# Four moves of small work in a fused forward-and-backward kernel: scalings of dO, sorted copies, the first FFT piece, and the order of tiles in pass two

## The chip, the cores and the metric

The kernel runs on one core of one Trainium2 chip. The metric is the time of one execution on the device in microseconds (us), the median of several runs; lower is better. A core has five engines with instruction streams of their own, each executed in order: PE (TensorE, matrix products), DVE (VectorE), ACT (ScalarE), POOL (GpSimd) and SP (SyncE). SP, POOL and ACT also issue DMA transfers. Engines wait for one another through semaphores.

## What is computed

The reference is a forward pass and its gradient. The input x has 2048 rows and 576 columns; the hidden width is F = 4608.

```python
g = sigmoid((x * gate_w).sum(-1, keepdims=True))
a = irfft2(rfft2(x) * (w_r + 1j * w_i))              # spectral branch A
b = (gelu(x @ w_gate) * (x @ w_up)) @ w_down         # gated branch B
out = g * a + (1 - g) * b
# returned: out, and the gradients of sum(out * grad_out) for
# x, w_r, w_i, w_gate, w_up, w_down, gate_w
```

Both branches read the same x; the input B_x is not used. Below, dO is `grad_out`.

## The kernel before, in words

**Tiling.** The 2048 rows are T = 16 row tiles of 128. The hidden width is cut into NG = 18 groups of 256 columns (`FG`). x, dO and their transposes (`xn`, `dB`, `xT`, `dOT`) stay in on-chip memory.

**Pass one** has 18 groups of four steps. A step (g, m) handles row tiles 4m to 4m+3 of group g; its number is `pr` = 4g + m, from 0 to 71, so the "fifth step" is pr 4. In each step PE first computes z = dO w_downᵀ (`H_mm`, lines 462 and 467) into a PSUM tile `z`. ACT copies z out in four instructions scaled by 1 - g (`H_da`, line 490, tile `da`). PE then computes x w_gate and x w_up in two halves (`xy_full`, lines 471 and 478), and ACT copies each half in three instructions (`H_act`, lines 497, 499 and 500, tiles `q`, `xb`, `hu`). DVE forms the gelu and its derivative in `H_ew1` and `H_ew2` (lines 505 to 546), with sigmoids on ACT (lines 525, 528, 529). The results A and dH are stored to DRAM scratch (`scr`) through SP.

**W products.** Behind its own products each step runs a share of the weight-gradient products of the group before (`W_units`): `u_dwd` (line 590: A by dB, for w_down) and `u_dw` and `tail` (lines 608 and 622: xn by dH). PSUM pool `pw` has two buffers `wps`; ACT copies them out (line 559). `u_dwd` needs dB scaled row by row with 1 - g. That is `scale_dB(k, engine)`: four instructions for row tiles 4k to 4k+3, on DVE (line 979) or ACT (line 977). Quarters 0, 1 and 2 are scaled in step 4, quarter 3 in step 5, ahead of two `build_R`.

**FFT pieces.** The transforms of x and dO are cut into units in the list `fft`, taken out in order by `fft_next()`. For each of 16 row tiles of x, and then of dO, there is a first unit `u1` (line 652: six products of the sorted row `xq` with a table `Rt`; ACT copies `Z` out, line 655 or 657) and a second `u2` (line 666; ACT copies `ve` out, line 672; DVE folds, SP stores). All these products use `pftile()`, the same single PSUM buffer (pool `pz`, one buffer, tag "z") as the z of each step: a piece must wait for da, and the next step's z must wait for the piece's copy. `want(pr)` is how many units are due by the end of step pr: none until step 7, one there, three by step 8, then three a step. In a step, the first piece (`k0`) goes between the two row tiles of the second half of xy, the others among the W products at due places.

**Sorts.** `sort(dst, t)` is one ACT instruction that copies row tile t, its columns regrouped into six classes, into `xq` (lines 720 and 722; for dO it is scaled by g and reads `graw`, loaded by SP). Before, tiles 0, 1 and 2 of x are sorted in steps 5, 6 and 7 behind `H_act`; the others hang on every odd unit of the list (`sorted_after`), so ACT sorts directly behind that unit's copy.

**Pass two** reads A and dH back, transposed by DMA, as tiles `pin` (line 1142; pool of six), on SP. A job "b" (row tile t) is 72 products of A with `wd_all` for the forward output; "g" and "u" are 72 products each of dH with the transposed w_gate and w_up for the gradient of x, accumulated in the same pair of PSUM buffers (pool `pacc`, eight). The list `jobs` is g0, g1, ten b tiles, u0, u1, b10, and then g, u, b in turn. `load_wuT` (line 1175) loads w_up transposed in nine DMA transposes on SP, one at the start of each job from job 3 on (g0 is job 0); u0 is the first job that needs them. Between the blocks of 12 products of a job, `tick` lets pieces of the inverse transforms run (lines 1269 and 1279, copied out by ACT at lines 1271 and 1281); `posts` joins a finished b tile with its inverse transform on DVE.

Of the kernel before, what the change touches and what calls it, by code (L numbers as in the profile page):

```python
# [20 lines left out]
P, T = 128, 16  # L21
# [9 lines left out]
NG = FF // FG  # L31
# [260 lines left out]
def kernel(  # L292
# [194 lines left out]
    def H_da(g, m, z):  # L487
        da = ewt("da", g)
        for t in range(4):
            nc.scalar.activation(da[:, t, :], z[:, t % 2, t // 2, :], ACT.Copy, scale=omg32[:, 4 * m + t:4 * m + t + 1])  # L490
        return da
# [151 lines left out]
    def fwd_units(src, dst, scale):  # L643
        zs = {}
        CLS = (1, 2, 0, 5, 4, 3)

        def u1(t):
            def f():
                zps = pftile()
                row = src.pop(t)  # L650
                for k, r in enumerate(CLS):
                    nc.tensor.matmul(zps[0:96, k // 3, k % 3 * P:(k % 3 + 1) * P], lhsT=row[:, r], rhs=tb.Rt[t], start=True, stop=True)  # L652
                zs[t] = unit([2, 3 * P], name="Z")
                if scale is None:
                    nc.scalar.copy(zs[t][0:96], zps[0:96, :, 0:3 * P])
                else:
                    nc.scalar.activation(zs[t][0:96], zps[0:96, :, 0:3 * P], ACT.Copy, scale=scale)
            return f

        def u2(t):  # L660
            def f():
                Z = zs.pop(t)
                vps = pftile()
                w = 2 * LQ
                for k in range(6):
                    nc.tensor.matmul(vps[:, k // 3, k % 3 * w:(k % 3 + 1) * w], lhsT=Z[0:96, k // 3, k % 3 * P:(k % 3 + 1) * P],  # L666
                                     rhs=tb.F[0:96, k].rearrange("p c l -> p (c l)"), start=True, stop=True)
                Vt = half([2, DF], name="Vt")
                ve = unit([2, 3, 2, LQ], F32, name="ve")
                sd = unit([2, 3, 2, LQ], F32, name="sd")  # L670
                M = unit([6, 2, LQ], F32, name="vm")
                nc.scalar.copy(ve[:].rearrange("p b k c l -> p b (k c l)"), vps[:, :, 0:3 * w])
                lo, hi = ve[:, 0], ve[:, 1]
                V.tensor_tensor(sd[:, 0], lo, hi, op=ALU.add)
                V.tensor_tensor(sd[:, 1, :, 0], hi[:, :, 0], lo[:, :, 0], op=ALU.subtract)
                V.tensor_tensor(sd[:, 1, :, 1], lo[:, :, 1], hi[:, :, 1], op=ALU.subtract)
                e, o = sd[:, 0, 2], sd[:, 1, 2]
                for k, op in enumerate((ALU.add, ALU.subtract)):
                    V.tensor_tensor(M[:, k], sd[:, 0, 0], sd[:, 0, 1], op=op)
                    V.tensor_tensor(M[:, 4 + k, 1::-1], sd[:, 1, 0], sd[:, 1, 1], op=op)  # L680
                p_, m_ = M[:, 0], M[:, 1]
                for c, op in enumerate((ALU.subtract, ALU.add)):
                    V.scalar_tensor_tensor(M[:, 2, c], m_[:, c], 0.5, o[:, c], op0=ALU.mult, op1=op)
                V.scalar_tensor_tensor(M[:, 3], p_, -0.5, e, op0=ALU.mult, op1=ALU.add)
                up = Vt[:, :, 96:DF - 1].rearrange("p c (j l) -> p j c l", j=2)[:, :, :, 0:LQ]
                dn = Vt[:, :, 1:193].rearrange("p c (j l) -> p j c l", j=2)[:, :, :, 94:47:-1]
                V.tensor_tensor(Vt[:, :, 0:LQ], e, p_, op=ALU.add)
                V.scalar_tensor_tensor(Vt[:, 0, DF - 1:DF - LQ:-1], o[:, 0, 0:LQ - 1], -1.0, m_[:, 0, 0:LQ - 1], op0=ALU.mult, op1=ALU.subtract)
                V.tensor_tensor(Vt[:, 1, DF - 1:DF - LQ:-1], m_[:, 1, 0:LQ - 1], o[:, 1, 0:LQ - 1], op=ALU.subtract)
                for c in range(2):  # L690
                    V.scalar_tensor_tensor(up[:, :, c], M[:, 4:6, c], SIN60, M[:, 2:4, c], op0=ALU.mult, op1=ALU.add)
                for c, s_, op in ((0, -SIN60, ALU.add), (1, SIN60, ALU.subtract)):
                    V.scalar_tensor_tensor(dn[:, :, c], M[:, 4:6, c, 1:LQ - 1], s_, M[:, 2:4, c, 1:LQ - 1], op0=ALU.mult, op1=op)
                LD.dma_start(dst[:, t], Vt[:])
            return f
        return [u1(t) for t in range(T)], [u2(t) for t in range(T)]

    xq, gq, graw = {}, {}, {}

# [16 lines left out]
    def sort(dst, t):  # L716
        if t % 2 == 0:
            classes(dst, t // 2)
        if dst is xq:
            nc.scalar.copy(xq[t], xn[:, t, :].rearrange("p (q r) -> p r q", r=6))  # L720
        else:
            nc.scalar.activation(gq[t], graw[t // 2][:, t % 2].rearrange("p (q r) -> p r q", r=6), ACT.Copy, scale=g32[:, t:t + 1])
# [150 lines left out]
    VC, AC = V.tensor_copy, nc.scalar.copy  # L873
# [27 lines left out]

    early = {2 * T + 4 * k - 13: load_g(k) for k in range(T // 2)}

    def sorted_after(u, n):
        def f():
            u()
            sort(*n)
        return f
    fg = []
    for i, u in enumerate(zipped(*fwd_units(xq, scr_x, None)) + zipped(*fwd_units(gq, scr_g, SD2))):  # L910
        if i in early:
            fg.append(early[i])
        n = (i + 5) // 2
        fg.append(sorted_after(u, (xq, n) if n < T else (gq, n - T)) if i % 2 and n < 2 * T else u)
    mid = mid_units()
    fft = fg + [turned] + mid

# [16 lines left out]
    def ready():  # L934
        u = fft[fft_pos[0]]
        return not hasattr(u, "needs") or u.needs()

    n_mid = sum(1 for u in mid if not getattr(u, "noslot", False))
    n_slots = sum(1 for u in fft if not getattr(u, "noslot", False))
    mid_at = 4 * T + 8  # L940
    NPR = NT // 2
# [4 lines left out]
    def want(pr):  # L946

        n0 = FIRST[-1]
        if pr < len(FIRST):
            return FIRST[pr]  # L950

        def load(n):

            return n + 0.5 * min(max(n - mid_at, 0), n_mid)
        share = load(n0) + (load(n_slots) - load(n0)) * (pr + 1 - len(FIRST)) / (LASTP - len(FIRST))
        n = n0
        while n < n_slots and load(n + 1) <= share + 1e-9:
            n += 1
        return int(min(n, n_slots) + 1e-9)

    wgT_all = []

# [11 lines left out]
    def scale_dB(k, cp):  # L974
        for t in range(4 * k, 4 * k + 4):
            if cp == AC:
                nc.scalar.activation(dB[:, t, :], dB[:, t, :], ACT.Copy, scale=omg32[:, t:t + 1])
            else:
                V.tensor_scalar(dB[:, t, :], dB[:, t, :], omg32[:, t:t + 1], None, op0=ALU.mult)  # L979

    for g in range(NG):
# [3 lines left out]
        for m in range(NPR):  # L985
            pr = g * NPR + m
            n = want(pr) - done[0]
# [65 lines left out]
            else:  # L1053
                z, xy_full = H_mm(g, m)
                da = H_da(g, m, z)
                for f in inside:
                    f()
                xy = xy_full(0)
                if held:
                    held.pop()()  # L1060
                k0 = int(n > 0 and pr > 6 and ready())
                xy0 = xy
                H_act(0, xy0, tiles, 1)
                pcopy[0] = VC
# [4 lines left out]
                    H_act(1, xy, tiles, part)  # L1069
                if pr == 4:  # L1070
                    scale_dB(2, AC)
                elif pr == 5:
                    sort(xq, 0)
                elif pr == 6:
                    next(makeB)
                    sort(xq, 1)
                elif pr == 7:
                    sort(xq, 2)
                state += [*H_ew1(g, tiles, da), da]
                if pr == 4:  # L1080
                    scale_dB(0, VC)
                    scale_dB(1, VC)
                elif pr == 5:
                    scale_dB(3, VC)
                    build_R(nc, tb, unit, 8)
                    build_R(nc, tb, unit, 12)
                side_work(4.4)
# [54 lines left out]
        LD.dma_start_transpose(tl[:], scr[k][t // 4][t % 4][:, f0 * P:(f0 + FCB) * P])  # L1142
        return tl

    jobs = [("g", t) for t in range(2)] + [("b", t) for t in range(10)] + [("u", t) for t in range(2)] + [("b", 10)]
    for t in range(2, T):
        jobs += [("g", t), ("u", t)] + ([("b", t + 9)] if t + 9 < T else [])
    jobs[-2:] = [("x", T - 1)]
    seq = [(k, t, f0) for kind, t in jobs for k in ((1, 2) if kind == "x" else ("bgu".index(kind),)) for f0 in range(0, NFC, FCB)]
    loaded = {}  # L1150
# [28 lines left out]
    with tc.tile_pool(name="p2f", bufs=3, **kw) as p2f, \  # L1179
# [236 lines left out]
                x_out(t, h, pre, o1, LD)  # L1416

        for i, (kind, t) in enumerate(jobs):
            if i > 2 and wT_loads:
                load_wuT(*wT_loads.pop(0))  # L1420
            if kind == "b":
                b_job(t)
                posts()
            elif kind == "g":
                x_half(t, 1)
            elif kind == "u":
                x_half(t, 2)
                need(t)
                assert posted[0] > t
                x_end(t)  # L1430
            else:
                need(t)
                assert posted[0] > t
                gate_grad()
                x_last(t)
# [30 lines left out]
```

## Time and profile before

| what | value |
|---|---|
| runs shown | 1369.44, 1373.15, 1372.83 us; median 1372.83 |
| the profiled execution | 1370.35 us; span of its instructions 1368.5 us |
| granted TensorE clock | 1.00 |
| PE busy, 40 to 905 us (steps of pass one) | 859.22 of 865.00 us |
| PE busy, 920 to 1040 us (start of pass two) | 118.88 of 120.00 us |
| PE busy, 1040 to 1366 us (rest of pass two) | 324.70 of 326.00 us |
| ACT busy, 75 to 100 us | 22.91 of 25.00 us |
| DVE busy, 50 to 75 us | 23.85 of 25.00 us |
| sort of x: L720 ACT COPY, 16 of them | mean 998 ns |
| sort of dO: L722 ACT ACTIVATE, 16 of them | mean 1084 ns |
| DMA share, 920 to 1040 us | 1.13 |

"Busy" is the time in which an engine has an instruction of its own in work. PE's products overlap one another in the pipeline, so the duration of one product is longer than the distance from its start to the next: a product of 512 columns has a duration of 380 ns, while 24 of them take 5.18 us in the chain of waits, 216 ns each. Where this text speaks of lost time on PE, it is worked out from the starts in the timeline and from these distances, not from durations.

### The profile page before, as it was taken

How to read it: one execution, taken by the hardware profiler on the slowest of the kernel's cores; microseconds unless marked ns; L12 is line 12 of the kernel's file. 1: busy time of each engine (PE TensorE's matmuls, PEld its weight loads, DVE VectorE, ACT ScalarE, POOL GpSimd, SP SyncE). 2: the span in 40 equal slices, each digit the busy share in tenths (PEclk: the TensorE clock that was granted, in tenths of full speed). 3: DMA queues.
4: the chain of work that ended last, by engine and by line, in shares of the span. 5: the costliest groups of instructions: out<-in, count | busy, mean ns of one | idle time of the engine just before them, and what ended most of it. 6: DMA issues, size and time to landing. Idle time of an engine off the chain costs nothing.

```text
span 1368.5 us, 27031 instructions
## 1 busy us (share of the span) xinstructions
PE 1355.7 (99%) x10360; PEld 900.7 (66%) x10360; DVE 880.7 (64%) x2353; ACT 772.9 (56%) x1378; POOL 245.1 (18%) x488
## 2 busy tenths in 40 slices
PE   9899999999999999999999999999999999999999
PEld 6456656656655655655655655558887888888887
DVE  7968888888857967876876755525535443545320
ACT  6788887887767776776777666622332322223210
POOL 3011111111222633433433311000000000000000
PEclk9999999999999999999999999999999999999999
DMA  8624435444454644644644657499999888778773
GB/s 224 173 62 136 124 109 153 122 128 128 130 144 117 169 122 132 169 117 120 175 127 126 162 119 183 119 262 205 197 203 216 173 161 169 160 161 175 151 151 75
DMA packets 493465, 206.90 MB, mean 151 GB/s; under 512 B 313332, under 2 KB 485303, under 8 KB 493335
## 3 DMA queue, kind: packets, MB, share of 16 engines
q1 hardware_dynamic: 467188, 170.32, 54.5%
q0 software_dynamic: 15040, 24.38, 6.3%
q10 hardware_dynamic: 11106, 10.48, 3.2%
q8 instruction: 81, 1.33, 0.4%
q14 instruction: 50, 0.40, 0.1%
HBM read 41.04 MB, written 89.11 MB: 95 GB/s over the span
## 4 chain that ended last, share of the span: by engine, by line
PE 94%; DVE 2%; ACT 2%; DMA 1%; issue 0%; SPq 0%; POOL 0%; ACTq 0%; DVEq 0%; POOLq 0%
PE acc L1216 30%; PE xy L478 17%; PE wps L608 17%; PE wps L590 10%; PE z L462 9%; PE wps L622 2%; PE xy L471 2%; PE z L467 2%; PE pf L652 1%; PE acc L1269 1%; DMA wuT<-in_B_w_up_dram 1%; PE acc L1279 1%; PE pf L849 1%; PE pf L771 1%; PE pf L666 1%; DMA pin<-scr 0%
## 5 line engine op out<-in xcount | busy, mean ns | idle before, releaser
L1216 PEld LDWEIGHTS <-pin 128*128 128x128 bf16 x3456 | 334.7, 98 | 85.2 <-issue 2.4
L478 PE MATMUL xy<-wgu,xT 128*128 128x512 bf16 x1152 | 270.5, 380 | 0.0
L608 PE MATMUL wps<-dH,xn 128*128 128x512 bf16 x1152 | 265.3, 379 | 0.0
L608 PEld LDWEIGHTS <-xn 128*128 128x128 bf16 x1152 | 111.3, 98 | 125.7 <-issue 0.6
L478 PEld LDWEIGHTS <-xT 128*128 128x128 bf16 x1152 | 105.6, 98 | 133.1 <-issue 25.9
L590 PE MATMUL wps<-dB,A 128*128 128x288 bf16 x1152 | 150.5, 286 | 3.2 <-DVE dB L979 3.2
L1216 PE MATMUL acc<-wuT,pin 128*128 128x288 bf16 x1152 | 146.4, 286 | 1.4 <-DMA wuT<-in_B_w_up_dram 1.0
L615 POOL DMA_DIRECT2D out_dram<-dw x134 | 72.6, 545 | 416.2 <-ACT dw L559 404.3
L1216 PE MATMUL acc<-wd_all,pin 128*128 128x288 bf16 x1152 | 146.9, 286 | 0.0
L1216 PE MATMUL acc<-wgT,pin 128*128 128x288 bf16 x1152 | 146.6, 286 | 0.0
L1281 ACT ACTIVATE yo<-acc 128x288 bf16<-128x288 f32 x64 | 67.4, 1246 | 132.9 <-PE acc L1279 121.5
L462 PE MATMUL z<-wdT,dOT 128*128 128x256 bf16 x1152 | 137.7, 273 | 0.8 <-DMA wdT<-in_B_w_down_dram 0.7
L590 PEld LDWEIGHTS <-A 128*128 128x128 bf16 x1152 | 111.8, 98 | 36.8 <-issue 4.0
L490 ACT ACTIVATE da<-z,omg 128x256 bf16<-128x256 f32 x288 | 111.9, 471 | 34.7 <-PE z L467 34.6
L462 PEld LDWEIGHTS <-dOT 128*128 128x128 bf16 x1152 | 112.3, 98 | 22.6 <-DMA wdT<-in_B_w_down_dram 1.2
L1397 DVE TENSOR_TENSOR b16t<-acc,f32t 128x288 bf16<-128x288 f32 x32 | 14.7, 458 | 172.9 <-PE acc L1216 172.8
L499 ACT CAST xb<-xy 128x512 bf16<-128x512 f32 x144 | 84.8, 589 | 48.6 <-PE xy L478 47.9
L1271 ACT CAST Z<-acc 98x384 bf16<-98x384 f32 x64 | 27.5, 481 | 106.1 <-PE acc L1269 106.1
L500 ACT CAST hu<-xy 128x512 bf16<-128x512 f32 x144 | 87.0, 604 | 0.0
L497 ACT ACTIVATE q<-xy 128x512 bf16<-128x512 f32 x144 | 80.0, 600 | 3.3 <-PE xy L478 3.3
L536 DVE TENSOR_TENSOR xb<-xb,sg 128x1024 bf16<-128x1024 bf16 x48 | 33.2, 691 | 74.3 <-ACT sg L528 74.3
L559 ACT CAST dw<-wps 128x512 bf16<-128x512 f32 x72 | 42.2, 588 | 48.2 <-PE wps L608 37.0
(515 smaller groups left out, 1811.2 us busy)
## 6 DMA issues: line engine op xcount, KB each, us to landing
scr<-dH SPq DMA_DIRECT2D x144, 256.0 KB, 3.5
scr<-A SPq DMA_DIRECT2D x72, 256.0 KB, 2.6
out_dram<-dw POOLq DMA_DIRECT2D x134, 64.0 KB, 1.9
wd_all<-in_B_w_down_dram SPq DMA_DIRECT2D x3, 1728.0 KB, 13.8
out_dram<-dwd POOLq DMA_DIRECT2D x34, 144.0 KB, 2.7
scr_p<-Vt SPq DMA_DIRECT2D x32, 144.5 KB, 3.4
Vp<-scr_p ACTq DMA_DIRECT2D x32, 144.5 KB, 4.4
wgu<-in_B_w_gate_dram SPq DMA_DIRECT2D x18, 256.0 KB, 4.2
```

Source lines behind the costliest of these rows:

```text
L462: nc.tensor.matmul(zo(t), lhsT=dOT[:, ci, t, :], rhs=wdT[:, ci, :], start=(t % 4 < 2 and ci == 0), stop=False)
L478: nc.tensor.matmul(xy[k][:, t % 2, :], lhsT=xT[:, ci, t, :], rhs=wgu[:, ci, :], start=False, stop=(ci == 3))
L490: nc.scalar.activation(da[:, t, :], z[:, t % 2, t // 2, :], ACT.Copy, scale=omg32[:, 4 * m + t:4 * m + t + 1])
L497: nc.scalar.activation(q[:, h, :], xy[:, :, 0:FG], ACT.Square)
L499: nc.scalar.copy(xb[:, h, :], xy[:, :, 0:FG])
L500: nc.scalar.copy(hu[:, h, :], xy[:, :, FG:2 * FG])
L559: wcopy[0](out, in_)
L590: nc.tensor.matmul(wps[:, :288], lhsT=tl(0, t)[:, fch * P:(fch + 1) * P], rhs=dB[:, t, h * 288:(h + 1) * 288], start=(t == 0), stop=(t == ...
L608: nc.tensor.matmul(wps[:].rearrange("p a b -> p (a b)"), lhsT=xn[:, t, c * P:(c + 1) * P], rhs=kt[t // 4][1][:, t % 4].rearrange("p k f -> ...
L615: wst[0].dma_start(ov[:, c, fsl], dw[:, k, :])
L1216: nc.tensor.matmul(acc[:, :288], lhsT=src[:, r, :], rhs=w_of(r)[:, h * 288:(h + 1) * 288], start=(first and r == 0), stop=(last and r == F ...
L1281: nc.scalar.activation(yv[:, 3 * b:3 * b + 3], ps[:, 0:288].rearrange("p (r q) -> p r q", r=3), ACT.Copy, scale=(SD2, 1.0)[w])
```

## The change

It makes five edits. (1) `scale_dB(3, VC)` moves from step 5 to step 4, so that DVE scales quarters 0, 1 and 3 there in one go. (2) The sorts leave the units and steps 5 to 7; `sort_ahead(pr)` runs directly behind `H_da` of each step and sorts every row tile whose first unit is due in the next step. (3) The first piece of step 7 no longer goes between the halves of xy (`pr > 7` instead of `pr > 6`) but among the W products. (4) Twelve b tiles instead of ten stand ahead of u0. (5) Jobs 5 and 11, counted from 0, load no part of w_up.

```diff
-        return [u1(t) for t in range(T)], [u2(t) for t in range(T)]
+        first = [u1(t) for t in range(T)]
+        for t, u in enumerate(first):
+            u.sort = (src, t)
+        return first, [u2(t) for t in range(T)]
...
-    def sorted_after(u, n):
-        def f():
-            u()
-            sort(*n)
-        return f
...
-        n = (i + 5) // 2
-        fg.append(sorted_after(u, (xq, n) if n < T else (gq, n - T)) if i % 2 and n < 2 * T else u)
+        fg.append(u)
...
+    slots = [u for u in fft if not getattr(u, "noslot", False)]
+    sorted_to = [0]
+
+    def sort_ahead(pr):
+        to = want(pr + 1) if pr + 1 < NG * NPR else n_slots
+        for u in slots[sorted_to[0]:to]:
+            if hasattr(u, "sort"):
+                sort(*u.sort)
+        sorted_to[0] = max(to, sorted_to[0])
...
                 da = H_da(g, m, z)
+                sort_ahead(pr)
...
-                k0 = int(n > 0 and pr > 6 and ready())
+                k0 = int(n > 0 and pr > 7 and ready())
...
-                elif pr == 5:
-                    sort(xq, 0)
                 elif pr == 6:
                     next(makeB)
-                    sort(xq, 1)
-                elif pr == 7:
-                    sort(xq, 2)
                 state += [*H_ew1(g, tiles, da), da]
                 if pr == 4:
                     scale_dB(0, VC)
                     scale_dB(1, VC)
+                    scale_dB(3, VC)
                 elif pr == 5:
-                    scale_dB(3, VC)
...
-    jobs = [("g", t) for t in range(2)] + [("b", t) for t in range(10)] + [("u", t) for t in range(2)] + [("b", 10)]
+    jobs = [("g", t) for t in range(2)] + [("b", t) for t in range(12)] + [("u", t) for t in range(2)] + [("b", 12)]
     for t in range(2, T):
-        jobs += [("g", t), ("u", t)] + ([("b", t + 9)] if t + 9 < T else [])
+        jobs += [("g", t), ("u", t)] + ([("b", t + 11)] if t + 11 < T else [])
...
-            if i > 2 and wT_loads:
+            if i > 2 and i % 6 != 5 and wT_loads:
```

In the order of instructions of the two built programs, every engine has the same work before and after. Step 6 and step 7 hold one sort each; the steps from 8 to 27 hold two and one in turn (two in every even step), all behind da.

## The prediction

> **What bounds the kernel now.** I read the page first, its busy times and the shares of the chain that ended last.
>
> ```profile
> PE 1355.7 (99%) x10360; PEld 900.7 (66%) x10360; DVE 880.7 (64%) x2353; ACT 772.9 (56%) x1378; POOL 245.1 (18%) x488
> ...
> PE 94%; DVE 2%; ACT 2%; DMA 1%; issue 0%; SPq 0%; POOL 0%; ACTq 0%; DVEq 0%; POOLq 0%
> ```
>
> PE is the bound and hardly ever stands still: 1368.5 - 1355.7 = 12.8 us of the span, of which the start and the end take some 4.7 (first product at 1.37 us, last end 3.3 us before the span's). No edit removes products, so the change can only gain what PE waits for, or add waits. The view of PE's waits says for what (waiter, releaser, total us, times, longest):
>
> ```profile
> PE wps L590 <- DVE dB L979: 3.2, 1, 3.2
> ...
> PE acc L1216 <- DMA wuT<-in_B_w_up_dram: 1.0, 1, 1.0
> PE pf L652 <- ACT da L490: 0.9, 1, 0.9
> PE pf L652 <- ACT ve L672: 0.8, 4, 0.2
> ...
> PE acc L1216 <- DMA pin<-scr: 0.4, 1, 0.4
> ```
>
> Each edit stands against one of these rows. I price them from the starts in the timeline, since a wait costs more than its idle time. Distances without a wait: 0.1225 us for a product of 288 columns (48 in 5.88 us in the chain), 0.216 for one of 512.
>
> **Edit 1, dB.**
>
> ```profile
> 59.74 2.61 PE L590 MATMUL wps<-dB,A 128*128 128x288 bf16 x20
> 65.58 2.10 PE L590 MATMUL wps<-dB,A 128*128 128x288 bf16 x12 [3.23 <-DVE dB L979]
> 67.52 1.91 PE L462 MATMUL z<-wdT,dOT 128*128 128x256 bf16 x16
> ```
>
> Twenty products need 20 x 0.1225 = 2.45 us, so the next was due at 62.19 and came at 65.58: 3.39 lost. The last twelve took 1.94 us instead of 1.47, because DVE frees dB tile by tile: 0.47. Together 3.86. In DVE's timeline the eight scalings of step 4 run from 55.94 to 58.17, when the next instruction starts, 0.28 us each; the four of step 5 start only at 65.17, behind the gelu of two steps. Moved up, they end at about 59.3, and PE wants them at 62.2: the wait is gone. Everything behind them on DVE comes 4 x 0.29 = 1.2 us later in step 4 and is level again where they stood. The sigmoid of step 5 waits for that DVE chain: it could start at 65.5 instead of 68.01 (it stood behind a copy that waited for PE), so ACT still moves up. Gain 3.86.
>
> What is late next? DVE's chain in steps 5 and 6 has no idle time to give and ends only some 0.6 us earlier (73.4 against 74.0), while PE is 3.9 ahead. Its consumer on ACT, the sigmoid of step 6, waits behind the two table loads and six sine instructions that begin with ACT's copy at 77.98; DVE's input to it ends at 77.5, the sigmoid starts at 84.76. That slack of 7 us covers it. If it did not, up to 3.3 of the 3.86 would come back.
>
> By the Trainium skill (TensorE: Matmul & The Clock Gate, "What's actually happening") an idle window of about 3.4 us halves PE's clock; a pause of 3.23 us lies just under it. The granted clock is 1.00 in the stretch from 50 to 75 us, so nothing is added here; by the rule at most one window at half speed, an estimate of 1.7 us, would be gained on top.
>
> **Edit 3, the first piece of step 7.**
>
> ```profile
> 83.69 2.76 PE L478 MATMUL xy<-wgu,xT 128*128 128x512 bf16 x12
> 87.32 0.49 PE L652 MATMUL pf<-Rt,xq 128*96 128x128 bf16 x6 [0.86 <-ACT da L490]
> ```
>
> In later steps the piece starts 2.60 after such a row begins (94.57 to 97.17), here 3.63: 1.03 lost, since da was late behind the tables. Four products of 512 later (0.86 us) it would barely have fitted, and the sort that goes from ahead of ACT's copy at 77.98 helps by half a microsecond: gone, +1.03. But there is a new wait. The piece's copy Z now stands on ACT behind da (1.42), one sort (0.9), and six copies of xy (about 2.9), before 0.8 of its own: some 0.5 us after PE wants to write the z of step 8 into the same buffer. PE's next instructions all stand behind that z. Bounds: 0, if da is early, to 1.5. I take 0.5.
>
> **Edit 2, the sorts.** Step 11, PE and ACT:
>
> ```profile
> 137.66 1.89 PE L608 MATMUL wps<-dH,xn 128*128 128x512 bf16 x8
> 139.70 0.49 PE L652 MATMUL pf<-Rt,xq 128*96 128x128 bf16 x6
> ```
> ```profile
> 135.69 1.00 ACT L720 COPY xq<-xn 128x576 bf16<-128x576 bf16 x1
> 136.59 1.07 ACT L497 ACTIVATE q<-xy 128x512 bf16<-128x512 f32 x2
> ...
> 138.97 0.68 ACT L672 COPY ve<-pf 128x588 f32<-128x588 f32 x1
> ```
>
> Eight products need 1.73 us, so the piece was due at 139.39; it waited 0.31 for ve, which ended at 139.65. The sort at 135.69 takes 0.90 of ACT's line ahead of it. Behind da it falls into 0.69 us in which ACT idled for xy, so ve ends about 0.9 earlier. Every fourth step has the same wait: at 139.70, 191.44, 243.25, 295.07 and 346.88, by the same count 0.31, 0.32, 0.39, 0.40, 0.39. Gain 1.8.
>
> The other side: in even steps two sorts (1.8 us, for dO 2.0) now stand ahead of the copies of xy, and behind those wait the pieces' copies, each of which the next piece on PE needs. In steps 10, 14, ... ACT idles 1.46 us there for xy, so little is pushed. Steps 12, 16, 20, 24 are tight: ACT idles only 0.21 (146.29). ACT's line is 1.6 later; ve ends at about 149.4, wanted at 149.82; Z ends at about 152.0, wanted at 151.88. So 0.1 to 0.3 lost in each, 0.7 in all. Bounds: 0, and one sort (0.9) in each of the ten two-sort steps, 9 us.
>
> By the Trainium skill (ScalarE: Activation LUTs, "What ACT_TABLE_LOAD costs") such an instruction of 576 columns would take 186 + 0.833 x 576 = 666 ns. The rows say 998 and 1084 (regrouped reads), and the measurement decides; by the page all the sort terms would shrink by a third.
>
> **Edits 4 and 5, pass two.**
>
> ```profile
> 1037.33 1.14 PE L1216 MATMUL acc<-wuT,pin 128*128 128x288 bf16 x8
> 1039.45 2.12 PE L1216 MATMUL acc<-wuT,pin 128*128 128x288 bf16 x16 [0.97 <-DMA wuT<-in_B_w_up_dram]
> 1042.01 1.65 PE L1216 MATMUL acc<-wuT,pin 128*128 128x288 bf16 x12 [0.45 <-DMA pin<-scr]
> ```
> ```profile
> 948.79 2.98 SPq L1175 DMA_TRANSPOSE wuT<-in_B_w_up_dram  x1
> ...
> 1031.52 3.98 SPq L1175 DMA_TRANSPOSE wuT<-in_B_w_up_dram  x1
> ```
>
> Lost at u0: 1.14 + 0.60 = 1.74. PE takes (1031.11 - 937.36) / 10 = 9.4 us per b tile. SP takes 10.6 with a w_up load (957.56 to 1031.52 is seven tiles) and, without its 3.8, 6.8. So SP falls back by 1.2 per tile: 2.1 us behind the start of its tile at the first load, 9.8 at the last. The last part lands 7.9 (the median) after issue, 17.7 after b9's start, and is wanted at 16.6. Now two tiles carry no load and give back 2.6 each: by the same count the lag is at most 8 and 6.6 at the last load, in b11, landing at 14.5, 2.1 us in time. Gain 1.74. Two short waits on PE among the b tiles, 0.30 (piece at 997.74) and 0.16 (row at 1020.07), come from ACT's own DMA issues standing still between such loads; I count 0.2 of them as gained. Two more tiles run while g0 and g1 hold four of eight PSUM buffers: the ten before lost 0.46 there, so at most 0.1 more.
>
> **Sum.** 3.86 + 1.03 + 1.81 + 1.74 + 0.2 - 0.5 - 0.7 - 0.1 = 7.3 us. The profiled execution took 1370.35 (span 1368.5 and 1.85 around it): 1363.0. The median of the runs is 2.5 higher and would give 1365.5. I take 1364.5.
>
> **The rivals.**
> - ACT and DVE can't follow the earlier PE in steps 6 to 8. For: DVE's chain gains only 0.6. Against: the 7 us of slack ahead of the sigmoid. 3.3 us come back: 1367.8.
> - Pass two keeps a wait at u0, because SP's lag is set by the DMA share (1.13 from 920 to 1040 us), not by the loads alone. Against: 2.1 us of margin. 1.7 come back: 1366.2.
> - The sorts land on the path, the slower end. Place: ACT between da and the copies of xy, in steps 8 to 27. If each of these 20 steps loses one sort of 0.9 to 1.0 us, 19 us are added and the 1.2 counted above for small waits fall away: 1364.5 + 19 - 1.2 = 1382. It decides from about 0.6 us per step on, since 7.3 + 4.1 us must be eaten. For: ACT is busy 22.91 of 25 us from 75 to 100. Against: it idles for xy in most steps, and the sorts removed stood in the same line a few instructions later.
> - The change moves waits without removing them (da late for the piece wherever it stands): 1.0 back, 1365.5, inside the range.
>
> **How the numbers follow.** What a measurement can tell is 0.3%, 4.1 us: faster is below 1368.7. Chances: forecast with its small variants 0.73; first rival 0.11; second 0.10; sorts on the path 0.06. Range 1361 to 1369.5: below, the gain without the new waits (8.6) from the lowest of the profiled and shown times, 1369.4; above, the first two rivals with the upper bound of the run-to-run spread. Faster 0.82 (the first rival falls on both sides of the line), same 0.12, slower 0.06.
>
> **What would show it.** PE's waits without DVE dB, without da at L652 and without wuT at u0; no wait for ve in steps 11, 15, ...; a new short wait of z (L462) for Z at about 87 us less 3.9. The span of PE from its first product to the end of step 71 should shrink by some 5.4, pass two by 1.9. Wrong would be: z or pieces waiting for ACT in most steps from 8 to 27, or u0 waiting for w_up again.

## The result, and the profile after

| | before | after |
|---|---|---|
| median of the runs | 1372.86 us (1369.44 to 1373.15, 4 runs) | 1364.03 us (1362.93 to 1364.56, 4 runs) |
| profiled execution | 1370.35 us, span 1368.5 | 1364.56 us, span 1362.8 |

The ratio of the times is 0.994, with a 95% interval of 0.9923 to 0.9958: faster, by 8.8 us between the medians. It was measured again later, on another chip, in more rounds: 1362.92 us against 1372.58, ratio 0.9929 [0.9916, 0.9941]. The forecast of 1364.5 holds. Between the two profiled executions the difference is only 5.8 us; why the medians are further apart is the main thing that the experiments had to settle.

First the page of the kernel after, its busy times and the shares of the chain that ended last:

```profile
PE 1355.2 (99%) x10360; PEld 901.8 (66%) x10360; DVE 880.8 (65%) x2353; ACT 770.1 (57%) x1378; POOL 246.0 (18%) x488
...
PE 96%; ACT 2%; DVE 1%; DMA 1%; issue 0%; SPq 0%; ACTq 0%; DVEq 0%
```

The work of every engine is what it was; only the span is shorter, and DVE's share of the chain fell from 2% to 1%. The view of PE's waits (waiter, releaser, total us, times, longest):

```profile
PE pf L881 <- POOL ident masks.py:199: 1.4, 1, 1.4
PE pf L433 <- DMA dB<-in_grad_out_dram: 1.2, 1, 1.2
PE acc L1210 <- ACT dw L559: 0.4, 1, 0.4
PE pf L666 <- ACT Z L657: 0.4, 2, 0.2
PE xy L471 <- ACT hu L500: 0.3, 1, 0.3
PE z L462 <- DMA scr<-A: 0.3, 1, 0.3
```

Gone are all five rows of the kernel before that the prediction named: dB, da, ve, wuT and pin. New are the second pieces' wait for Z and one of z (L462), whose releaser is misnamed, as an experiment shows. The first two rows belong to the start of the program, which no edit touches.

PE's timeline in step 4 shows the 20 + 12 products of before as one row, without a pause; DVE's shows the twelve scalings in one go (start, us, engine, line, operation, count):

```profile
61.45 4.08 PE L590 MATMUL wps<-dB,A 128*128 128x288 bf16 x32
65.37 1.91 PE L462 MATMUL z<-wdT,dOT 128*128 128x256 bf16 x16
```
```profile
58.06 3.44 DVE L986 TENSOR_SCALAR dB<-dB,omg 128x576 bf16<-128x576 bf16 x12
```

And step 11, which the prediction showed with its wait for ve, PE and ACT:

```profile
134.86 1.89 PE L608 MATMUL wps<-dH,xn 128*128 128x512 bf16 x8
136.59 0.50 PE L652 MATMUL pf<-Rt,xq 128*96 128x128 bf16 x6
```
```profile
129.83 0.48 ACT L490 ACTIVATE da<-z,omg 128x256 bf16<-128x256 f32 x1
130.19 1.02 ACT L723 COPY xq<-xn 128x576 bf16<-128x576 bf16 x1
...
135.32 0.66 ACT L672 COPY ve<-pf 128x588 f32<-128x588 f32 x1
```

The sort stands behind da, ve ends 0.6 us before the piece, and the piece follows its eight products after 1.73 us, which is their unstalled distance.

Where the time went, stretch by stretch. Every product loads weights, and the starts of these loads are recorded without a gap in every profile (10360 of them); counting them gives the same point of the work in two programs. A point is named below by its time in the first profile of the kernel before. (Some later profiles lack records of a few dozen products, so that PE's busy time there is short by some 7 us.)

| stretch, by the times of before | before, us | after, us | difference | predicted |
|---|---|---|---|---|
| 0 to 45.05, the start | 45.05 | 46.75 | +1.70 | none |
| to 80.02, steps 3 to 6 | 34.97 | 31.11 | -3.86 | -3.86 (dB) |
| to 95.01, steps 7 and 8 | 14.99 | 14.41 | -0.58 | -1.03 + 0.5 |
| to 905.07, the rest of pass one | 810.06 | 809.27 | -0.79 | -1.81 + 0.7 |
| to the last load at 1364.74, pass two | 459.67 | 457.44 | -2.23 | -1.74 - 0.2 + 0.1 |

Without the first row it is 7.46 us, where 7.34 were forecast. The first row doesn't look like the change's doing: no edit touches that stretch, and in twelve other profiles the same point lies at 44.6 to 47.0 us, with no relation to the edits that shows: 46.79 in a second profile of the kernel after, 45.20 in one with edit 5 undone. The windows of after show one stretch at half speed there, from 7.95 to 11.36 us, that the profiled execution of before lacks (start and end, us, busy us and instructions of PE, PEld, DVE, ACT and POOL, granted clock as a share of TensorE's full speed, DMA share, GB/s):

```profile
4.54:7.95 3.41, 2.13 (x34) 1.65 (x32) 1.41 (x3) 0.96 (x4) 1.99 (x6) 1.00 0.95 289
7.95:11.36 3.41, 3.41 (x28) 2.88 (x26) 0.68 (x2) 1.01 (x1) 0.00 (x0) 0.50 1.10 369
```

In the window before it PE stood still for a load of dO (the 1.2 in the waits). In both measurements of the kernel after, the profiled execution is the slowest and the only one with a mean granted clock of 0.999; the other seven have 1.000 and took 1362.4 to 1364.3 us. So the two profiled executions differ by the change and by what happened at the start.

### The profile page after: what moved, and what is told of

The parts are those of the page before. It is cut to its first block, busy times and chain, and to the rows that moved or that the text cites. A ratio compares the mean times of both kernels' runs of the same rounds, so it can differ in the third digit from the quotient of the medians.

```text
span 1362.8 us, 27025 instructions
## 1 busy us (share of the span) xinstructions
PE 1355.2 (99%) x10360; PEld 901.8 (66%) x10360; DVE 880.8 (65%) x2353; ACT 770.1 (57%) x1378; POOL 246.0 (18%) x488
## 4 chain that ended last, share of the span: by engine, by line
PE 96%; ACT 2%; DVE 1%; DMA 1%; issue 0%; SPq 0%; ACTq 0%; DVEq 0%
PE acc L1219 31%; PE xy L478 17%; PE wps L608 17%; PE wps L590 10%; PE z L462 9%; PE wps L622 2%; PE xy L471 2%; PE z L467 2%; PE acc L1272 1%; PE pf L652 1%; PE pf L666 1%; PE acc L1282 1%; PE pf L852 1%; PE pf L774 1%; DMA dB<-in_grad_out_dram 0%; ACT da L490 0%
## 5 line engine op out<-in xcount | busy, mean ns | idle before, releaser
L462 PE MATMUL z<-wdT,dOT 128*128 128x256 bf16 x1152 | 138.6, 274 | 0.3 <-DMA scr<-A 0.3
L462 PEld LDWEIGHTS <-dOT 128*128 128x128 bf16 x1152 | 112.8, 98 | 22.1 <-issue 0.6
## 6 DMA issues: line engine op xcount, KB each, us to landing
wd_all<-in_B_w_down_dram SPq DMA_DIRECT2D x3, 1728.0 KB, 14.9
```

What stands on the lines that cost most here:

```text
L462: nc.tensor.matmul(zo(t), lhsT=dOT[:, ci, t, :], rhs=wdT[:, ci, :], start=(t % 4 < 2 and ci == 0), stop=False)
```

## The experiments

Each kernel ran beside runs of the kernel before on the same chip; ratios are against those.

**The kernel before, unchanged (before_again).**

> The kernel before, unchanged, for a second profile. Between the two profiled executions the change gained 5.8 us (1370.35 to 1364.56), between the medians 8.8. Theory A: the executions of the kernel before differ by how long u0 waits for w_up, since SP's lag of 9.8 us stands just past the point from which PE waits; then a profile here that takes about 1373 shows more than 1.7 us lost at u0 and the same 3.9, 1.0 and 1.8 elsewhere. Theory B: they differ at the start, in the first 45 us, where loads are awaited; then the difference stands there. Theory C: it is spread over all stages.

Measured: 1372.84 us against 1372.58, ratio 1.0001 [0.9991, 1.0011]; profiled 1373.87 us, span 1372.1. Its waits:

```profile
PE wps L590 <- DVE dB L979: 3.6, 1, 3.6
PE acc L1216 <- DMA pin<-scr: 2.1, 2, 1.2
...
PE acc L1216 <- DMA wuT<-in_B_w_up_dram: 0.7, 1, 0.7
```

In pass two it took 461.41 us from 905.07's point to the last load, 1.74 more than the first profile: PE waits now 0.7 for w_up and 2.1 for pin, 3.3 us by starts against 1.74. So the wait at u0 varies from execution to execution of the kernel before, as the theory had it. But 3.5 us separate the two profiled executions, and pass two has half of it. The other half stands in two views, the timeline of PE and the windows from 63.65 us on:

```profile
65.69 2.68 PE L590 MATMUL wps<-dB,A 128*128 128x288 bf16 x12 [3.64 <-DVE dB L979]
68.16 3.04 PE L462 MATMUL z<-wdT,dOT 128*128 128x256 bf16 x16
```
```profile
60.23:63.64 3.41, 1.82 (x15) 1.31 (x14) 3.36 (x6) 2.28 (x4) 0.53 (x2) 1.00 0.75 191
63.65:67.06 3.41, 1.37 (x8) 0.72 (x8) 3.33 (x8) 0.21 (x1) 0.00 (x0) 1.00 0.63 186
67.06:70.47 3.41, 3.41 (x17) 2.34 (x16) 2.23 (x5) 1.54 (x3) 0.54 (x1) 0.50 0.08 32
70.47:73.88 3.41, 3.41 (x48) 2.48 (x46) 3.34 (x7) 1.57 (x4) 0.00 (x0) 1.00 0.05 16
```

The sixteen products of z take 3.04 us where the first profile had 1.91. For exactly 3.41 us after the pause for dB the granted clock is 0.50. From the first product behind the pause to a fixed point after it (69 weight loads) PE takes 8.30 us here and 6.63 in the first profile: 1.67 us that the wait's own length doesn't contain.

**Edit 1 alone (dB_alone).**

```diff
                     scale_dB(1, VC)
+                    scale_dB(3, VC)
                 elif pr == 5:
-                    scale_dB(3, VC)
```

> The kernel before with only the fourth quarter of dB scaled in step 4. Mine: 3.9 us less than the kernel before, and no wait for DVE dB. Rival (ACT and DVE cannot follow the earlier PE): PE waits again in steps 6 to 8, for da at L652 above all, longer than the 0.86 us before, and 0.6 to 2 us are gained.

Measured: 1367.58 us (1366.56 to 1369.33), ratio 0.9967 [0.9955, 0.9979], 5.0 us less by medians; span 1364.7. Its waits:

```profile
PE pf L652 <- ACT ve L672: 1.0, 5, 0.2
PE pf L652 <- ACT da L490: 0.9, 1, 0.9
PE acc L1216 <- DMA wuT<-in_B_w_up_dram: 0.8, 1, 0.8
```

The wait for dB is gone, the others stay as they were: nothing of it comes back behind ACT or DVE, and the first rival falls. The surplus over 3.9 is of the size of the clock's term. The executions with a mean granted clock of 1.000 bear that out: the five of dB_alone took 1367.4 us in the mean and the three of the kernel before beside it 1370.8, only 3.4 more. In this profile the sigmoid of step 6 starts at 81.05, 4.3 us after DVE's input to it ends (76.71).

**Edits 4 and 5 alone (pass2_alone).** The kernel before with the new list of jobs and the skipped loads.

> The kernel before with only twelve b tiles and the two jobs without a load of w_up. Mine: no wait for w_up at u0 and no short waits behind ACT among the b tiles, 1.7 to 2.2 us less in the profile. If theory A on the kernel before holds, 3 to 5 us less by the medians. Rival (SP stays behind because the DMA share is full): a wait for w_up or pin of a microsecond remains at u0, less than 1 us gained.

Measured: 1369.69 us, ratio 0.9979 [0.997, 0.9988], 2.9 us less; span 1366.2. PE waits neither for wuT nor for pin, and pass two takes 457.44 us, as in the kernel after. This profile also shows what the pause for dB hides: it came to 45.05's point 1.05 us later than the first profile (a wait for w_down), waited only 2.1 us for dB, and resumed at 65.52 against 65.58. So in the kernel before a late start can be swallowed by that pause; without the pause it is paid.

**Edits 2 and 3 alone (sorts_alone).** The kernel after with `scale_dB`, the jobs and the loads of before.

> The kernel before with only the sorts behind da and the first piece of step 7 among the W products. Mine: the five waits for ve and the one for da gone (1.8 and 1.0), four waits of 0.2 to 0.4 for Z in steps 12 to 24 and one of about 0.4 ahead of the z of step 8 in their place: 1.3 to 1.9 us less. Rival (sorts on the path): no gain or a loss.

Measured: 1369.98 us, ratio 0.9983 [0.9974, 0.9992], 2.6 us less; span 1367.0. The waits for da and ve are gone; z of step 8 waits (0.46 us lost), and the second pieces of steps 12, 16, 20 and 24 wait for Z (0.16, 0.15, 0.35 and 0.35). Between the trace's points of 80.02 and 905.07 it takes 823.63 us where before takes 825.06, a gain of 1.43; the rest of the 2.6 by medians is not attributed.

**The kernel after again (after_again).**

> The changed kernel once more, for a second profile and as the measure of the three kernels timed beside it. Mine: 1362.5 to 1365 us; again four waits for Z in steps 12, 16, 20 and 24 (0.2 for x, 0.35 for dO by start distances) and one of about 0.4 ahead of the z of step 8, and no wait in pass two behind the first products. Its runs should spread less than the kernel before's, since the wait at u0 that varied there is gone.

Measured: 1362.92 us (1362.42 to 1364.48), ratio 0.9929 [0.9916, 0.9941]; span 1362.7. The same small waits, Z 0.4 in two and z 0.3.

**Second sorts later (late_second).** The second sort of steps 12, 16, 20 and 24, and the sort of step 7, move from ahead of the copies of xy to behind the first piece among the W products.

```diff
+    later = []
+
     def sort_ahead(pr):
+        n_sorted = 0
...
-                sort(*u.sort)
+                if pr == 7 or (pr % NPR == 0 and pr > 8 and n_sorted):
+                    later.append(u.sort)
+                else:
+                    sort(*u.sort)
+                n_sorted += 1
...
+                        if later:
+                            sort(*later.pop())
```

> The changed kernel, but in steps 12, 16, 20 and 24 the second sort, and in step 7 the only one, goes behind the first piece among the W products. Theory: the five small waits left in steps 7 to 24 are those of a copy Z that stands behind a sort; then they go (0.17 + 0.17 + 0.36 + 0.38 + 0.44 = 1.5 us) and nothing takes their place, since before the change a sort stood there too: 1.0 to 1.5 us less than the changed kernel. Rival: the sort delays ve there and the next step's z waits instead; no gain.

Measured: 1362.07 us (1361.14 to 1363.32), ratio 0.9919 [0.9906, 0.9933]. PE's timeline in step 12, of the kernel after and then of this one:

```profile
147.05 1.89 PE L608 MATMUL wps<-dH,xn 128*128 128x512 bf16 x8
148.95 0.43 PE L666 MATMUL pf<-Ft,Z 96*128 96x98 bf16 x6
```
```profile
146.88 1.89 PE L608 MATMUL wps<-dH,xn 128*128 128x512 bf16 x8
148.61 0.43 PE L666 MATMUL pf<-Ft,Z 96*128 96x98 bf16 x6
```

Eight products need 1.73 us. The piece comes 1.90 after them in the one (0.17 lost) and 1.73 in the other. All five new waits are gone and nothing takes their place; between the points of 80.02 and 905.07 it takes 822.18 us where after takes 823.68. The medians differ by 0.9, with overlapping intervals: the trace shows the gain, the runs alone don't. It is the best version here.

**Edit 3 undone (first_piece_back).** The kernel after with `pr > 6` in place of `pr > 7`.

> The changed kernel with the first piece of step 7 between the halves of xy again. Mine: da, without the sort ahead of the table loads, is 0.4 to 0.6 us late for the piece there (it was 0.86 to 1.03), and Z is early enough for step 8, so the wait of 0.44 ahead of its z goes: within 0.3 us of the changed kernel. Rival (the move was worth the 1.03 us by itself): 1 us slower.

Measured: 1363.59 us, ratio 0.9932 [0.992, 0.9945]. The piece of step 7 waits for da (0.63 us lost) in place of z's 0.44, and from 80.02's point to 905.07's it takes 823.81 us against 823.68. With the sorts gone from ahead of it, edit 3 by itself is worth 0.1 us in the trace, which the runs can't show.

**Each sort done twice (sorts_twice).** The kernel after with 32 further sorts on ACT, each directly behind the first of its kind.

> The changed kernel with every sort done twice, so that ACT has 32 more instructions of 1.0 us behind da; the result is the same. It measures how near the rival of the sorts on the path was. Mine: steps 12, 16, 20 and 24 lose nearly the full two sorts (1.9 us each), steps 10, 14, 18, 22 and 26 some 0.4, steps 11 to 27 of the one-sort kind 0.3 or less, step 8 one: 8 to 14 us more than the changed kernel. If ACT had room enough: under 2 us more. If the sorts lay on the path everywhere: 29 us more.

Measured: 1379.91 us against 1371.03, ratio 1.0059 [1.0044, 1.0074]; span 1377.7, 14.9 over after's. Its waits:

```profile
PE pf L652 <- ACT ve L672: 8.0, 9, 1.8
...
PE pf L666 <- ACT Z L655: 2.3, 5, 1.1
PE pf L666 <- ACT Z L657: 1.6, 4, 0.4
...
PE z L462 <- ACT Z L655: 1.3, 1, 1.3
```

From 80.02's point to 905.07's it takes 840.36 us, 16.7 more than after, for 16 x 0.90 + 16 x 1.0 = 30.4 us more of ACT's line (start to start, as the sorts stand in the profile of before). More was lost than expected: ACT's idle time in these steps holds the sorts once, and of a second helping over half lands on PE. The last row is the z of step 8, now with its true releaser, the copy Z; that is the row that the kernel after prints as "DMA scr<-A".

**Twelve b tiles, no load skipped (twelve_no_skip).** The kernel before with edit 4 alone.

> The kernel before with twelve b tiles, but a load of w_up in each job from 3 to 11. Mine: the last part is issued 9.8 us behind b9 and is wanted only 35 us behind it, so no wait for w_up; of the waits for pin and behind ACT among the b tiles 0 to 0.8 us may stay: 2.0 to 2.9 us less than the kernel before by the medians, nearly what both edits of pass two gave together. Rival (the two jobs without a load do it): a wait of a microsecond at u0 stays.

Measured: 1371.2 us (1369.29 to 1373.43), ratio 0.999 [0.998, 1.0]: 1.4 less by medians, where more was expected. Yet its profile shows no wait at u0, and pass two takes 457.44 us, the same as with the skip; the last part of w_up lands at 1040.00 and u0 begins at 1051.92. What this profiled execution lost, it lost elsewhere: the clock is at 0.50 for two windows behind the pause,

```profile
61.89:65.30 3.41, 0.55 (x5) 0.29 (x3) 3.27 (x7) 1.00 (x2) 0.00 (x0) 1.00 0.92 241
65.30:68.71 3.41, 2.62 (x11) 1.45 (x11) 3.31 (x9) 0.40 (x1) 0.00 (x0) 0.50 0.28 81
68.71:72.12 3.41, 3.41 (x18) 2.30 (x16) 1.83 (x4) 1.35 (x2) 0.54 (x1) 0.50 0.11 43
```

and the 69 loads take 9.15 us against 6.63. What the skip is worth had to be seen without that noise (after_no_skip, below).

**The pause made longer (dB_after_tables).** The kernel before with `scale_dB(3, VC)` behind the two `build_R` of step 5.

> The kernel before with the fourth quarter of dB scaled behind the two build_R of step 5 instead of ahead of them, so that PE's pause grows from 3.2 to about 5.5 us. If a pause costs itself alone: 2.2 us more than the kernel before. If a pause beyond 3.4 us halves PE's clock for a while, as the rule has it: the granted clock in the stretch from 60 to 80 us falls below 1, the products behind the pause start at twice their distance, and up to 1.7 us come on top.

Measured: 1373.96 us against 1371.03 on this chip, ratio 1.0019 [1.001, 1.0029], 2.9 us more; the pause is 5.70 us. PE's timeline:

```profile
60.23 2.61 PE L590 MATMUL wps<-dB,A 128*128 128x288 bf16 x20
68.54 3.15 PE L590 MATMUL wps<-dB,A 128*128 128x288 bf16 x12 [5.70 <-DVE dB L979]
71.49 3.39 PE L462 MATMUL z<-wdT,dOT 128*128 128x256 bf16 x16
```

A longer pause costs its length, and here the clock behind it is 0.50 for 6.8 us again (67.7 to 74.5): the 69 loads take 9.13 us, 2.50 more than at full clock. Up to 80.02's point this profile is 4.97 us behind the first one of the kernel before, counted from 45.05's: 2.47 of pause and 2.50 of clock.

**The pause filled with work (idle_filled).** The kernel before, with the first twelve products of the waiting dB tile done a second time, ahead of the four that wait. PE has more to do; the result is the same.

```diff
-                for t in range(8 * half, 8 * half + 8):
+                twice = (g, fch, h, half) == (0, 0, 0, 1)
+                n_ = [False, twice]
+                for t in [8, 9, 10, 11] * twice + [0, 1, 2, 3, 4, 5, 6, 7] * twice + list(range(8 * half, 8 * half + 8)):
...
-                                     rhs=dB[:, t, h * 288:(h + 1) * 288], start=(t == 0), stop=(t == T - 1))
+                                     rhs=dB[:, t, h * 288:(h + 1) * 288], start=(t == 0), stop=(t == T - 1 or (t == 11 and n_.pop())))
```

> The kernel before with 12 more products on PE: the first 12 of the 16 products of the first dB tile of step 4's W products are done a second time, ahead of the four that wait for quarter 3 (12 x 0.1225 = 1.47 us of extra work; the result is the same). Theory C, the clock: in most executions of the kernel before the pause for dB is long enough to bring the granted clock to 0.50 for one or two stretches of 3.4 us behind it (profiles: 1.00 throughout after a pause of 3.23; half clock for 3.4 us after 3.64, and the products behind it 1.67 us later than at full clock). With the pause filled to some 1.8 to 2.2 us the clock stays at 1.00 from 60 to 80 us, the mean granted clock is 1.000 in nearly all executions, and the median falls by 1.0 to 2.0 us although PE does more: about 1371 beside 1372.5. The wait itself still ends at 65.5. Rival, the executions of before differ through pass two alone: no change, or some tenths more, and the mean clocks stay between 0.997 and 0.999.

Measured: 1371.55 us against 1372.45, ratio 0.9994 [0.9986, 1.0003]: not resolved, and less than expected. Five of twelve executions have a mean granted clock of 1.000, against 2 of 17 of the kernel before beside it, not nearly all. Those five took 1370.33 to 1371.07 us and the other seven 1371.29 to 1375.53. The profile shows why the expectation was too simple:

```profile
65.70 2.40 PE L592 MATMUL wps<-dB,A 128*128 128x288 bf16 x12 [1.89 <-DVE dB L981]
```
```profile
63.95:67.36 3.41, 1.66 (x10) 0.95 (x10) 3.38 (x9) 0.40 (x1) 0.00 (x0) 1.00 0.57 160
67.36:70.78 3.42, 3.42 (x18) 2.40 (x17) 2.53 (x5) 1.35 (x2) 0.54 (x1) 0.50 0.11 43
```

The clock is 0.50 from 67.36 to 70.78 here too, after a pause of only 1.89 us; in the first profile of before a pause of 3.23 us did not bring it down. The windows run on through a whole trace: in before_again the two falls of the clock, at 67.06 and at 1370.95 us, lie 382 windows of 3.4133 us apart. So the fall at the end of the first profile of before, at 1368.05, gives the places of its windows too:

```profile
60.74:64.15 3.41, 1.61 (x14) 1.16 (x12) 3.27 (x6) 1.66 (x3) 0.00 (x0) 1.00 0.97 217
64.15:67.57 3.42, 1.99 (x13) 1.21 (x13) 3.35 (x10) 0.40 (x1) 0.00 (x0) 1.00 0.47 136
```

Its pause (62.35 to 65.58) was split between two windows, 1.80 and 1.43 us; here all but 0.14 of the 1.89 lies in one. So the length of the pause alone does not decide, and where the windows lie matters. PE's busy time in the window gives no clean border either: after 1.66 us the clock fell here, after 1.61 it stayed at 1.00 there, and at the start of the kernel after it fell after 2.13. What the clock goes by stays open.

**Edit 5 undone (after_no_skip).** The kernel after without `i % 6 != 5`.

> The changed kernel with a w_up load in every job from job 3 on, none skipped (edit 5 undone). Theory: twelve b tiles are enough by themselves (the profile of the kernel before with twelve tiles and no skip shows no wait at u0), so the skip is worth nothing: 1362.9 to 1363.6, no wait for wuT or pin in pass two. Rival: nine loads in a row leave SP so late that in many executions u0 or a b tile waits: 0.8 to 1.5 us more than the changed kernel, 1364 to 1365, with a wider spread.

Measured: 1364.62 us (1363.0 to 1367.62, 6 runs), ratio 0.9948 [0.9936, 0.9961]. Three of the six executions took over 1365 us; of nine of the kernel after none did. My theory, that the skip is worth nothing, is not borne out, though the interval of the ratio overlaps with those of the kernel after. In the profiled execution (span 1362.3) the last part of w_up lands at 1033.64, and u0 begins at 1044.83, so it isn't u0 that is late. What is late is ACT: its timeline here, and that of the kernel after at the same place,

```profile
988.49 0.34 ACTq L1326 DMA_DIRECT2D x_t<-in_A_x_dram  x1
...
989.92 0.34 ACTq L1326 DMA_DIRECT2D do_t<-in_grad_out_dram  x1
993.00 0.33 ACTq L1233 DMA_DIRECT2D Vp<-scr_p  x1
993.37 0.40 ACT L1342 CAST bo<-acc 128x288 bf16<-128x288 f32 x1 [4.20 <-DMA do_t<-in_grad_out_dram]
```
```profile
990.06 0.34 ACTq L1326 DMA_DIRECT2D x_t<-in_A_x_dram  x1
...
990.44 0.45 ACTq L1326 DMA_DIRECT2D do_t<-in_grad_out_dram  x1
991.00 0.36 ACTq L1233 DMA_DIRECT2D Vp<-scr_p  x1
```

From the first of the three issues to the last ACT's queue takes 4.5 us here and 0.9 in the kernel after; the copy bo behind them comes late, and PE loses 1.06 us at 993.83. Such triples of issues come five times from 940 to 1050 us in every profile. In each of the six profiles with the skip the longest of the five took 1.1 to 1.9 us, in each of the eight without it 2.3 to 5.8. So the skip keeps ACT's queue moving; that is not always worth time on PE, since twelve_no_skip (longest 2.27) lost none in pass two. Why the queue stands still was not tested, and whether the executions over 1365 us lose more of the same was not traced.

## Why the prediction was right, and where it was not

**The bound and the sum.** PE was the bound, and the gain is what it waited for. The forecast terms came to 7.34 us, and by the trace the stretches gained 7.46.

**dB, 3.86.** It measured 3.86 between the profiled executions. DVE's four further scalings delayed nothing that PE needs, and of the slack of 7 us ahead of step 6's sigmoid 4.3 were left (dB_alone). The step that failed is the one on the clock: "The granted clock is 1.00 in the stretch from 50 to 75 us, so nothing is added here". That was true of the one execution that I had. Of 73 executions of the kernel before, run beside the experiments, 8 have a mean granted clock of 1.000, of 35 in which dB doesn't wait (both measurements of the kernel after, dB_alone, late_second, first_piece_back, sorts_twice, after_no_skip) 29. Where a profile shows the half clock, the 69 loads behind the pause took 1.38 (sorts_alone), 1.67 (before_again), 2.50 (dB_after_tables) and 2.52 us (twelve_no_skip) more than at full clock; the estimate that the prediction weighed there was 1.7. So edit 1 was worth 3.9 in the profiled pair and 5.0 between the medians (dB_alone). The clock is not all of the spread: of the 73, the 8 at 1.000 took 1370.8 us in the mean and the 65 others 1372.6, but on one of the four chips (beside sorts_twice) the four at 0.997 took no longer than the two at 1.000 (1370.7 and 1371.1).

**First piece of step 7, 1.03 - 0.5.** 0.58 was measured. The new wait of z for Z came where it was expected and cost 0.44. The rival that waits only move would have left all of the 1.03 ungained; 0.44 of it did move.

**Sorts, 1.81 - 0.7.** 0.79 was measured. The five waits for ve are gone (step 11 above). The waits for Z were put at 0.1 to 0.3 each in steps 12, 16, 20 and 24; by starts they lost 0.17, 0.17, 0.36 and 0.38, so 1.08 and not 0.7. The two later ones are in steps that sort dO, which takes ACT longer than x (1084 and 998 ns). The slower rival, sorts on the path, did not come, but sorts_twice shows that the room it needs is small.

**Pass two, 1.74 + 0.2 - 0.1.** 2.23 was measured against the first profile, 4.0 against the second, since u0's wait in the kernel before is not one number. The waits of the pieces for ACT among the b tiles vanished altogether (0.46, of which 0.2 were counted), and more PSUM pressure didn't show. The last load of w_up lands at 1047.36 in the kernel after and is wanted near 1052.2, 4.8 us in time where 2.1 were reckoned. The reasoning gave too much to edit 5 in one place and too little in another: u0 doesn't need the skip, but ACT's issues are held up without it, at a cost to PE in one of two profiles (1.06 us and nothing). The rival that kept a wait at u0 falls.

**The median.** I set 1364.5 between 1363.0 (from the profiled execution) and 1365.5 (from the median). The excess of before's median over its profile was taken as common to both kernels. That was wrong at least in part: half clock behind the pause and longer waits at u0 are before's own and go away with the change; the profiled after came out at 1364.56 with its late start. The medians were 1364.03 and then 1362.92, both nearer to 1363.0 than to 1365.5; that 1364.5 came within half a microsecond of the first one is partly luck. The mechanisms were right, and the sizes that were off are dB's in most executions, the Z waits and pass two.

## What to carry to other kernels

A pause of the bounding engine costs its length and can cost clock behind it, and whether one profile shows the second part is chance: compare the mean granted clock of many executions before a pause is priced from one trace. Compare two profiles stretch by stretch between the same points of the work, so that the start's luck is not taken for the change's effect. When small work is moved on an engine off the bound, look for the step in which that engine idles least, since that is where the new wait comes; and a load that itself is early can still hold up the DMA issues of another engine.

## What the runs showed of the hardware

- The granted clock falls to 0.50 in whole stretches of 3.41 us, one or two at a time, on a raster that runs through the whole trace. In the window of 3.41 just before the stretch behind the pause for dB, PE was busy 0.00, 0.27, 0.55, 1.37 and 1.66 us (dB_after_tables, sorts_alone, twelve_no_skip, before_again, idle_filled), and 2.13 and 2.10 us before the stretch at the start of the two profiles of the kernel after. It stayed at 1.00 after windows near the pause with 1.61 and 1.99 (the first profile of before), 1.82, 1.92 and 1.97 us. So busy time, by the durations in the trace, does not by itself say when it falls. The stretch ended after a window with PE busy all through, and went on after windows with 2.57 and 2.62 us. The Trainium skill (TensorE: Matmul & The Clock Gate, "What's actually happening") has the clock fall after one idle window of about 3.4 us that runs free of the program. The length and the free running agree with these runs; that the window must be idle does not, since 1.66 us of work in it did not keep the clock.
- A product of 256 columns follows the last one after 109 ns at full clock; sixteen of them took 1.91 us, and 3.39 at 0.50. Of the twelve products behind the pause for dB the first four, which DVE's scalings pace, came 0.28 us apart at either clock; the later ones came 0.12 us apart at full clock and 0.24 at 0.50.
- A DMA issue on ACT's queue took 0.3 to 0.4 us, yet 3.1 us passed between two of them (989.92 to 993.00) with w_up loaded in every job (after_no_skip), and 0.56 at the same place in the kernel after.
